# The first load of a decode kernel, w1, issued as two loads: 16 partitions and 112

## The chip, the cores and the metric

The kernel runs on one core of a Trainium2 chip. Its time is the device time of one execution in microseconds; the figure before the change is the median of three runs, 343.58 us (343.47 to 343.65). The profile is of one more execution, taken by the hardware profiler.

A core has a matrix engine (TensorE, PE in the profile; PEld is its weight load), a vector engine (VectorE, DVE), a scalar engine (ScalarE, ACT), a general one (GpSimd, POOL) and a sequencer that here only issues transfers (SyncE, SP). Transfers from device memory (HBM) into the on-chip memory (SBUF, 128 partitions) are run by 16 DMA engines. Each queue of transfers, such as SP's, spreads a transfer over them.

## The reference

One decode step for two sequences (B = 2, one new token each, model width 512). A gate mixes an attention block and a feed-forward block:

```
g = sigmoid((x * gate_w).sum(-1))                       # one number per sequence
q = x @ wq                                              # 512 -> 32 heads x 128
p = softmax(q . k_cache^T / sqrt(128))                  # 32 heads, 4096 cached rows each
a = (p @ v_cache) @ wo                                  # 4096 -> 512
b = relu(x @ w1) @ w2                                   # 512 -> 1376 -> 512
out = g * a + (1 - g) * b
```

All inputs are bfloat16. The K cache and the V cache hold 2 x 32 x 4096 x 128 numbers, 67 MB each; wq and wo have 4 MB each, w1 and w2 1.4 MB each. Every byte is read once.

## The kernel before, in words

The program is written engine by engine. A small class collects, for each engine, a list of operations with the markers or load semaphores they wait for; nothing is reordered afterwards, so every engine and every queue works in the order in which its list was filled.

SBUF holds one large tile `kv` of five regions (A, Ah, B, Bh, C), each 128 partitions of 16,384 bfloat16. Everything large that is loaded passes through it. A *piece* is a half region or two halves of a K or V unit: 4096 KB in one region or 8192 KB in two (128 partitions with one contiguous run of 32 or 64 KB each). w1 lies at the head of region B (128 partitions, 4 x 1376 numbers each, 11,008 bytes), wq in region C.

SP's list is, in order: w1 (L331), wq (L332), ten pieces of K and nine of V (L335), the 96 rows of w2 that don't fit the regular form (L338, two loads of 12 partitions each), wo in two loads (L340, L342), the rest of w2 in three loads (L344), and at the end the store of the result (L346). A load waits on SP until the last reader of its region is done. The first ones need no wait: w1, wq, the first half unit of K (region Bh) and the next unit (regions A and Ah). The third piece goes to region B and waits for the last matmul that reads w1 (marker `pe_h`); the fourth goes to region C and waits for `pe_q`, the end of the projection that reads wq. ACT's queue issues two tiny loads at the start, x (two partitions, L329) and the gate's row (one partition, L330).

The work at the start: PE turns x and the gate's row (function `gate`, L353), and a chain of short DVE and ACT operations computes the gate. `ffn_h` (L445 and after) clears a PSUM area on DVE and then runs 24 matmuls of x against w1, the first of which waits for w1's semaphore and for the clear. `ffn_relu` follows on DVE. `q_proj` waits for wq, computes q, turns it and lays it out (ACT copies, then POOL products). After that the K loop runs: DVE transposes a quarter piece as soon as the piece has landed (L477), PE takes the scores (L504, L483). Softmax, the V loop (L617, L483), and the output projections with w2 and wo follow.

Loads and compute are tied by counting semaphores. A load adds 16 to its semaphore when it is complete; w1's semaphore is `sem["w1"]`, and the only one who waits for it is the first matmul of `ffn_h`.

Of the kernel before, what the change touches and what calls it, by code (L numbers as in the profile page):

```python
# [122 lines left out]
def bass_gated_mix__gqa_block_cached__dense_activation_relu__decode_kernel(  # L123
# [34 lines left out]
    w1 = kv[:, REGION["B"]:REGION["B"] + 4 * DFF]  # L158
# [41 lines left out]
    def psf(p0, p1, c0, n):  # L200
        return PSF[p0:p1, c0:c0 + n]
# [22 lines left out]
    sem = {n: nc.alloc_semaphore("sem_" + n) for n in names}  # L224
# [9 lines left out]
    def marker(name):  # L234
        m = mk.get(name)
        if m is None:
            m = _Marker()
            mk[name] = m
        return m
# [29 lines left out]
    def dve(fn, waits=(), signal=None, dwaits=()):  # L269
        P.add("dve", fn, waits=[marker(w) for w in waits], signal=marker(signal) if signal else None, dwaits=dwaits)  # L270

    def act(fn, waits=(), signal=None, dwaits=()):
        P.add("act", fn, waits=[marker(w) for w in waits], signal=marker(signal) if signal else None, dwaits=dwaits)

    def pe(fn, waits=(), signal=None, dwaits=()):
        P.add("pe", fn, waits=[marker(w) for w in waits], signal=marker(signal) if signal else None, dwaits=dwaits)
# [5 lines left out]
         waits=["c_i16z"], signal="c_i16")  # L282
# [11 lines left out]
         waits=["c_s1"], signal="c_s2")  # L294
    pool(lambda g: g.affine_select(out=sell_odd, in_=sell_odd, pattern=[[4, 8], [32, 4]],
                                   compare_op=ALU.is_ge, fill=0.0, base=3, channel_multiplier=-1),
         waits=["c_s2"], signal="c_sell")
# [3 lines left out]
         waits=["c_m1"], signal="c_m2")  # L301
    pool(lambda g: g.affine_select(out=mask8[:], in_=mask8[:], pattern=[[16, 8]],
                                   compare_op=ALU.is_ge, fill=0.0, base=15, channel_multiplier=-1),
         waits=["c_m2"], signal="c_mask8")
# [3 lines left out]
         waits=["c_s4z"], signal="c_s4")  # L308
# [3 lines left out]
    w1_in = B_w1.rearrange("(p t) f -> p (t f)", t=4)  # L312
# [13 lines left out]
    def sp(fn, waits=(), dwaits=()):  # L326
        P.add("sp", fn, waits=waits, dwaits=dwaits)

    act(lambda e: e.dma_start(x_sb[0:2, :], A_x.rearrange("b s d -> (b s) d")).then_inc(sem["x"], 16))  # L329
    act(lambda e: e.dma_start(x_sb[2:3, :], gate_w.rearrange("(o d) -> o d", o=1)).then_inc(sem["gw"], 16))  # L330
    sp(lambda e: e.dma_start(w1, w1_in).then_inc(sem["w1"], 16))  # L331
    sp(lambda e: e.dma_start(wreg[:, :], wq_in).then_inc(sem["wq"], 16))  # L332
    for kind, n, u, halves, region in pieces:
        sp(lambda e, kind=kind, n=n, u=u, halves=halves, region=region:
           e.dma_start(piece_sb(halves, region), piece_in(kind, u, halves)).then_inc(landed[kind, n][0], 16),  # L335
           waits=[marker(m) for m in predecessor[kind, n]])
    for a in range(2):
        sp(lambda e, a=a: e.dma_start(w2x[32 * a:32 * a + 12, :, :].rearrange("p j n -> p (j n)"), w2x_in[a]).then_inc(sem["w2x"], 16),  # L338
           waits=[marker("c_w2x")])
    sp(lambda e: e.dma_start(wreg[:, 0:512 * WO_CUT], wo_in[:, 0:512 * WO_CUT]).then_inc(sem["wo0"], 16),  # L340
       waits=[marker(holder["C"][0])])
    sp(lambda e: e.dma_start(wreg[:, 512 * WO_CUT:HALF], wo_in[:, 512 * WO_CUT:HALF]).then_inc(sem["wo1"], 16))  # L342
    for name, r0, r1 in (("w2b", 0, 7), ("w2c", 7, 9), ("w2d", 9, 10)):
        sp(lambda e, name=name, r0=r0, r1=r1: e.dma_start(w2[:, r0:r1, :], w2_in[:, r0:r1, :]).then_inc(sem[name], 16),  # L344
           waits=[marker(holder["Ah"][0])])
    sp(lambda e: e.dma_start(out.rearrange("b s (k n) -> (b s k) n", k=2), out_sb[:, :]).then_inc(sem["out"], 16),  # L346
       dwaits=[(sem["fin"], 2)])
# [55 lines left out]
    def x_rows(e, out, c, t, rhs, held):  # L403
        if held:
            return mm_held(e, out, xTw[:, t, :], rhs, t == 0, t == 3, (128, 32), (0, 32 * c))
        return e.matmul(out, lhsT=xTw[:, t, :], rhs=rhs, start=(t == 0), stop=(t == 3), tile_position=(0, 32 * c))  # L406
# [37 lines left out]
    def ffn_h():  # L444
        dve(lambda v: v.memset(psf(0, 128, HR_C0, 448), 0.0), signal="dve_h0")  # L445
        for t in range(4):
            for c in range(4):
                def fn(e, t=t, c=c):
                    rhs = w1[:, t * DFF + 96 + 320 * c:t * DFF + 416 + 320 * c].rearrange("p (i j) -> p j i", j=10)
                    out = psf(32 * c, 32 * c + 32, HR_C0, 320).rearrange("p (j i) -> p j i", j=10)  # L450
                    return x_rows(e, out, c, t, rhs, False)
                first = t == 0 and c == 0
                pe(fn, dwaits=([(sem["w1"], 16)] if first else []), waits=(["dve_h0"] if first else []))
                if c < 2:
                    def fnx(e, t=t, c=c):
                        rhs = w1[:, t * DFF + 48 * c:t * DFF + 48 * c + 48].rearrange("p (i e j) -> p j e i", i=4, e=3)
                        out = psf(32 * c, 32 * c + 32, HR_C0 + 320, 128).rearrange("p (j k) -> p j k", j=4)[:, :, 0:12].rearrange(
                            "p j (e i) -> p j e i", e=3)
                        return x_rows(e, out, c, t, rhs, True)
                    pe(fnx)  # L460
        P.ops["pe"][-1].marker = marker("pe_h")
# [269 lines left out]

    gate()
    ffn_h()
    ffn_relu()
    q_proj()
# [73 lines left out]
```

## Time and profile before

| What | us |
|---|---|
| median of three runs | 343.58 |
| the profiled execution's own time | 343.51 |
| its span, first to last instruction | 342.2 |
| PE busy | 228.1 (67%) |
| DVE busy | 197.4 (58%) |
| ACT busy | 9.9 (3%) |
| POOL busy | 14.2 (4%) |
| issue of w1 on SP to its landing | 5.6 |
| issue of wq on SP to its landing | 14.8 |

The span is shorter than the execution's own time by what lies before the first and after the last instruction. An engine's busy time leaves out instructions that only issue a transfer; those appear in the timeline as SPq and ACTq, with the time that the issuing takes. "To landing" runs from the start of an issue to the moment when the load is complete. In a table by stretches, each row gives a stretch (start and end from the span's start, its length), the busy time and number of instructions of PE, PEld, DVE, ACT and POOL, the granted clock of TensorE as a share of full speed, the mean busy share of the 16 DMA engines and the GB/s that they moved. A packet's time and bytes are put down at the packet's start, so that share can go over 1 in a short stretch. Behind these tables lie the trace's packet records: start, length and bytes of every packet, with its queue but not with its engine.

### The profile page before, as it was taken

Reading aid. Unit: us, or ns where it says so; the run is one execution under the profiler, and the core shown is the slowest. Engines: PE = TensorE matmul, PEld = TensorE weight load, DVE = VectorE, ACT = ScalarE, POOL = GpSimd, SP = SyncE. Lnnn points to the kernel's source line nnn. Section 1 sums busy time; section 2 is a strip of 40 time slices with the busy share of each in tenths; the row PEclk is TensorE's granted clock in tenths of the full one; section 3 lists DMA queues with packets and bytes.
Section 4 is the critical chain, followed back from the end, with each engine's and each line's share of the span. In section 5 each row is a group of like instructions: output and inputs, shape, how many; then the busy total and the mean of one; then the engine's idle time right before and its main releaser. Section 6 shows DMA issues by size and latency. Waiting matters only on the chain.

```text
span 342.2 us, 2434 instructions
## 1 busy us (share of the span) xinstructions
PE 228.1 (67%) x1279; PEld 54.0 (16%) x770; DVE 197.4 (58%) x139; ACT 9.9 (3%) x29; POOL 14.2 (4%) x41
## 2 busy tenths in 40 slices
PE   0467329799969799689799463809172552909976
PEld 0111001111111111111111120202020110202313
DVE  1239059899889899698999496140606032020621
ACT  1051000000000000000000110000000000000000
POOL 6000000000000000000000200000000000000000
PEclk9999959989989899999999967856769585767999
DMA  8998989899999999898989999999989999989995
GB/s 349 429 490 370 483 375 483 371 486 414 444 467 391 426 433 483 383 475 375 483 383 475 398 467 423 429 467 391 483 383 475 391 467 391 467 387 433 426 421 241
DMA packets 3793, 145.50 MB, mean 425 GB/s; under 512 B 429, under 2 KB 564, under 8 KB 844
## 3 DMA queue, kind: packets, MB, share of 16 engines
q1 hardware_dynamic: 3782, 145.43, 98.6%
q8 instruction: 4, 0.07, 0.1%
q14 instruction: 1, 0.01, 0.0%
q10 hardware_dynamic: 6, 0.00, 0.0%
HBM read 145.43 MB, written 0.00 MB: 425 GB/s over the span
## 4 chain that ended last, share of the span: by engine, by line
DMA 63%; DVE 19%; PE 15%; issue 2%; ACT 0%; SPq 0%; DVEq 0%
DMA kv<-in_A_k_cache_dram 32%; DMA kv<-in_A_v_cache_dram 24%; DVE kt L477 17%; DMA kv<-in_B_w_dram 7%; PE PS L483 6%; PE PS L617 4%; PE PS L504 2%; PE PS L588 1%; DVE mpad L520 1%; ACT kt L532 0%; DVE kt L536 0%; DVE kt L549 0%; PE PS L697 0%; PE PS L516 0%; SPq L332 0%
## 5 line engine op out<-in xcount | busy, mean ns | idle before, releaser
L477 DVE STREAM_TRANSPOSE kt<-kv 128x2048 f32<-128x2048 f32 x64 | 141.2, 2274 | 25.7 <-DMA kv<-in_A_k_cache_dram 25.7
L504 PE MATMUL PS<-kt,qbuf 128*128 128x512 bf16 x256 | 106.2, 415 | 31.3 <-issue 23.0
L483 PE MATMUL PS<-kt,qbuf 128*128 128x512 bf16 x256 | 106.1, 415 | 0.0
L617 PE MATMUL PS<-kv,kt 128*64 128x512 bf16 x192 | 47.4, 471 | 55.2 <-DMA kv<-in_A_v_cache_dram 55.2
L629 DVE TENSOR_TENSOR kt<-PS,maskc 32x512 f32<-32x512 f32 (+1 forms) x21 | 14.5, 689 | 88.3 <-PE PS L483 81.3
L504 PEld LDWEIGHTS PS<-kt,qbuf 128*128 128x128 bf16 x256 | 25.7, 100 | 140.7 <-issue 140.7
L483 PE MATMUL PS<-kv,kt 128*64 128x512 bf16 x192 | 46.8, 465 | 0.0
L617 PEld LDWEIGHTS PS<-kv,kt 128*64 128x64 bf16 x192 | 15.2, 135 | 96.1 <-issue 96.1
L561 DVE TENSOR_TENSOR kt<-kt,mask 128x2048 bf16<-128x2048 bf16 (+1 forms) x10 | 16.2, 1656 | 0.0
L588 PE MATMUL PS<-kv,kt 128*32 128x512 bf16 x128 | 8.9, 432 | 8.6 <-DVE kt L549 7.3
L401 POOL TENSOR_TENSOR qbuf<-qs,mask 128x64 bf16<-128x64 bf16 x16 | 6.5, 406 | 160.7 <-PE PS L483 141.1
L641 DVE TENSOR_REDUCE kt<-kt 128x128 f32<-128x512 f32 x9 | 9.2, 1025 | 0.3
L483 PE MATMUL PS<-qbuf,ident 128*32 128x512 bf16 x37 | 9.0, 379 | 0.0
L406 PE MATMUL PS<-kv,xTw 128*32 128x320 bf16 (+1 forms) x32 | 5.3, 691 | 5.2 <-DMA kv<-in_A_wq_dram 3.2
L532 ACT ACTIVATE kt<-PS,negm 128x512 bf16<-128x512 f32 x4 | 2.7, 686 | 168.9 <-DVE negm L528 168.9
L588 PEld LDWEIGHTS PS<-kv,kt 128*32 128x32 bf16 x128 | 3.9, 107 | 15.6 <-DVE kt L549 7.8
L430 DVE CAST qrow<-PS 128x256 bf16<-128x256 f32 x2 | 2.6, 1524 | 5.7 <-PE PS L483 5.7
L729 ACT ACTIVATE out_sb<-PS 4x128 bf16<-4x128 f32 x1 | 0.3, 267 | 142.3 <-PE PS L712 142.3
L353 PE MATMUL PS<-ident,x_sb 3*128 3x3 bf16 x4 | 0.3, 166 | 6.2 <-DMA x_sb<-in_gate_w_dram 6.2
L520 DVE TENSOR_REDUCE mpad<-PS 128x2 f32<-128x2048 f32 x1 | 2.3, 2292 | 3.1 <-PE PS L516 3.1
L356 DVE COPY xT<-PS 128x12 bf16<-128x12 bf16 x1 | 0.2, 171 | 6.5 <-PE PS L353 6.5
L483 PE MATMUL PS<-kv,xTw 128*32 128x512 bf16 (+1 forms) x24 | 3.7, 511 | 0.0
(88 smaller groups left out, 53.6 us busy)
## 6 DMA issues: line engine op xcount, KB each, us to landing
kv<-in_A_k_cache_dram SPq DMA_DIRECT2D x4, 4096.0 KB, 29.4
kv<-in_A_v_cache_dram SPq DMA_DIRECT2D x2, 4096.0 KB, 23.5
kv<-in_A_wq_dram SPq DMA_DIRECT2D x1, 4096.0 KB, 14.8
kv<-in_A_wo_dram SPq DMA_DIRECT2D x1, 3072.0 KB, 33.4
kv<-in_B_w_dram SPq DMA_DIRECT2D x1, 1376.0 KB, 5.6
kv<-in_A_wo_dram SPq DMA_DIRECT2D x1, 1024.0 KB, 35.4
kv<-in_B_w_dram SPq DMA_DIRECT2D x1, 896.0 KB, 22.3
kv<-in_B_w_dram SPq DMA_DIRECT2D x1, 256.0 KB, 22.6
```

Source lines behind the costliest of these rows:

```text
L401: pool(lambda g: g.tensor_tensor(out=out, in0=src, in1=mask, op=ALU.mult).then_inc(sem_q[k % 2], 1), waits=waits)
L406: return e.matmul(out, lhsT=xTw[:, t, :], rhs=rhs, start=(t == 0), stop=(t == 3), tile_position=(0, 32 * c))
L477: dve(lambda v: v.transpose(out=dst, in_=pairs[:, h, 64 * a:64 * a + 64, :]).then_inc(sem_kt[i % SPAN], 1), waits=([f"pe_sc_{i - NKT}"] if ...
L483: return e.add_instruction(mybir.InstMatmult(start_tensor_calc=start, stop_tensor_calc=stop, tile_size=size, tile_position=at, ldweights=F ...
L504: ins = e.matmul(out, lhsT=lhsT, rhs=rhs, start=False, stop=False)
L520: dve(lambda v: v.tensor_reduce(out=mpad[:, 0:2], in_=psf(0, 128, 0, 4 * BANK).rearrange("p (par n) -> p par n", par=2), axis=AX.X, op=ALU ...
L532: act(lambda a, g=g, par=par: a.activation(out=E_sb[:, 32 * g:32 * g + 32, 16 * par:16 * par + 16], in_=psf(0, 128, (2 * par + g) * BANK, ...
L561: ins = v.tensor_tensor(out=out, in0=src.unsqueeze(2).to_broadcast(shape), in1=mask8[:].unsqueeze(1).unsqueeze(3).to_broadcast(shape), op= ...
L588: ins = e.matmul(psf(32 * t, 32 * t + 32, V_BS[n] * BANK, 512), lhsT=v_weights(n)[:, j], rhs=rows[:, :, j, :], start=(j < 4), stop=(j >= n ...
L617: ins = e.matmul(out, lhsT=lhsT, rhs=rows[:, :, k, :], start=start, stop=stop, tile_position=(0, 64 * t))
L629: dve(lambda e: e.tensor_tensor(out=parts[p0:p1], in0=psf(p0, p1, bank * BANK, 512).rearrange("p (c d) -> p c d", c=4), in1=maskc[p0:p1].u ...
L641: dve(lambda e: e.tensor_reduce(out=X2[:, b, k, :], in_=parts.rearrange("p c d -> p d c"), axis=AX.X, op=ALU.add), waits=[f"dve_m{n}"], si ...
```

## The change

The load of w1 is issued as two loads by SP, one right after the other: first partitions 0 to 15, then partitions 16 to 127. Source and destination rows are those of before; both loads add 16 to the same semaphore, and the matmul that waits for w1 waits for 32 instead of 16. As the change's author describes it, the first of the two is one packet for each DMA engine. All other issues keep their order behind these two.

```diff
     act(lambda e: e.dma_start(x_sb[0:2, :], A_x.rearrange("b s d -> (b s) d")).then_inc(sem["x"], 16))
     act(lambda e: e.dma_start(x_sb[2:3, :], gate_w.rearrange("(o d) -> o d", o=1)).then_inc(sem["gw"], 16))
-    sp(lambda e: e.dma_start(w1, w1_in).then_inc(sem["w1"], 16))
+    sp(lambda e: e.dma_start(w1[0:16], w1_in[0:16]).then_inc(sem["w1"], 16))
+    sp(lambda e: e.dma_start(w1[16:128], w1_in[16:128]).then_inc(sem["w1"], 16))
     sp(lambda e: e.dma_start(wreg[:, :], wq_in).then_inc(sem["wq"], 16))
...
                 first = t == 0 and c == 0
-                pe(fn, dwaits=([(sem["w1"], 16)] if first else []), waits=(["dve_h0"] if first else []))
+                pe(fn, dwaits=([(sem["w1"], 32)] if first else []), waits=(["dve_h0"] if first else []))
```

## The prediction

> **What bounds the kernel now.** I read the page's table of DMA queues first, because the kernel reads 145 MB.
>
> ```profile
> q1 hardware_dynamic: 3782, 145.43, 98.6%
> HBM read 145.43 MB, written 0.00 MB: 425 GB/s over the span
> ```
>
> The columns are packets, MB and the share of 16 DMA engines' span. The one queue that SP fills keeps all 16 engines busy for 98.6% of 342.2 us. Nothing else on the page comes near (PE 67%, DVE 58%), so bytes set the time, at 425/16 = 26.6 GB/s for each engine. I call one engine a lane: it works through its own part of every load in order, and a lane that starts late stays late: in the packet records the sixteen lanes finish w1 spread over 0.42 us, wq over 0.45 and the first K piece over 0.45.
>
> Next, whether a delay at the head reaches the end: the DMA issues, with size and median time from issue to landing, and the first long piece of the chain that ended last (start, length).
>
> ```profile
> kv<-in_B_w_dram SPq DMA_DIRECT2D x1, 1376.0 KB, 5.6
> kv<-in_A_wq_dram SPq DMA_DIRECT2D x1, 4096.0 KB, 14.8
> kv<-in_A_v_cache_dram SPq DMA_DIRECT2D x7, 28.5
> kv<-in_A_k_cache_dram SPq DMA_DIRECT2D x6, 28.4
> ```
>
> ```profile
> 1.72 24.08 DMA kv<-in_A_k_cache_dram
> ```
>
> A full K or V piece has 8192 KB, which is 19.7 us at 425 GB/s; it lands 28.4 us after its issue. So 8.7 us of older loads still lie in the queue at each issue, the engines never wait for SP, and a later start of the stream moves every landing, every release of a buffer and the end by the same amount. The start counts one for one.
>
> The start itself: first SP's timeline (start, length, instruction), then the stretches of the first 5 us (last two columns: DMA share and GB/s, both put down where a packet starts).
>
> ```profile
> 0.80 0.40 SPq L331 DMA_DIRECT2D kv<-in_B_w_dram  x1
> 1.26 0.41 SPq L332 DMA_DIRECT2D kv<-in_A_wq_dram  x1
> ```
>
> ```profile
> 1.70:1.80 0.10, 0.00 (x0) 0.00 (x0) 0.00 (x0) 0.10 (x1) 0.10 (x3) 1.00 0.07 21
> 1.80:2.20 0.40, 0.00 (x0) 0.00 (x0) 0.00 (x0) 0.40 (x1) 0.40 (x3) 1.00 1.49 275
> 2.20:3.00 0.80, 0.00 (x0) 0.00 (x0) 0.00 (x0) 0.71 (x1) 0.80 (x1) 1.00 0.64 220
> 3.00:4.00 1.00, 0.00 (x0) 0.00 (x0) 0.00 (x0) 0.00 (x0) 1.00 (x2) 1.00 1.01 429
> 4.00:5.00 1.00, 0.00 (x0) 0.00 (x0) 0.00 (x0) 0.00 (x0) 0.87 (x8) 1.00 0.96 407
> ```
>
> w1 is 128 rows of 11,008 bytes, a packet each, eight a lane. From 4 to 5 us 407 KB go, which is 37 packets in 0.96 x 16 us of lane time: 0.415 us a packet, 3.32 us for eight. The start is slower: from 1.80 to 3.00 us 110 + 176 KB start, 26 packets. Sixteen lanes at full pace from 1.80 would have started 48 (three each). The 22 missing are 1.4 a lane, 0.57 us. This is what the edit can work on.
>
> **The change, part by part.** The sum is against the profiled execution's 343.51 us (span 342.2 and 1.3 around it), which lies 0.07 below the median 343.58.
>
> *One more issue on SP.* 0.40 us and a gap of 0.06: wq, all K, V and later loads are issued 0.46 later. It costs nothing by itself: wq's packets have to wait for w1's, which fill the lanes to about 5.5 us, and wq's issue would move from 1.26 to 1.72. The first release that SP waits for is that of region B by the feed-forward matmuls at 13.0 us, so no one waits for SP.
>
> *The wait for w1 counts to 32.* One PE wait still, and it is not the last one: w1 lands at 0.80 + 5.6 = 6.4 us, while the first matmul of L406 starts at 10.12, released by the DVE memset at 9.64. Up to 3.7 us of delay of w1 are hidden there. Behind it PE has done at 12.95 and then waits for wq until 16.12, so 3.2 us cover the gate's row too, which comes between w1's packets. The waits later in the kernel are on loads that move along.
>
> *The first piece, 16 rows.* The bounds from rows are far apart. If each of 16 lanes takes one row at its own pace, it costs 0.415 us, what the same row costs now. The two rows of x, in neighbouring partitions, are the row for that: they start together in the stretch 1.70:1.80, and 0.07 x 16 x 0.10 us is some 0.11 us of lane time for both with their completions, 44 ns a row in the packet records, no slower than the 46 ns of a 1,024-byte packet of w2 late in the run. The other bound is the only load near in shape, w2's extra rows (L338: 12 partitions, twice 48 KB). The packet records show its 24 packets of 4,096 bytes from 325.05 to 326.48 us, three at a time, 156 ns apart in each row of eight: 12 partitions got three lanes' worth, 3 x 26.3 GB/s, four partitions to a lane. By that 16 partitions get four lanes' worth, and the piece takes 4 x 0.415 = 1.66 us instead of 0.415 (1.92 if I divide the 98,304 bytes by the whole 1.43 us and scale from 12 partitions to 16). I take 1.66: w2's extra rows are near in partitions (12 against 16) and in bytes (96 KB against 172), while x's 44 ns are too short to show a jam.
>
> [...]
>
> *The second piece, 112 rows.* Seven a lane would be 7 x 0.415 = 2.91 us. [...] So the whole of w1 on a full group goes from 3.32 to 1.66 + 3.32 us: **+1.66**.
>
> *The faster start.* The first piece has 16 packets to lay out instead of 128, so its lanes may start together and up to 0.1 earlier (x's first packet started at 1.71, w1's at 1.82). At most the 0.57 + 0.10 = 0.67 us of the slow start go; nothing goes if the second piece's packets come in the same slow manner 0.46 us later. I take the middle, **-0.33**, as there is no row of a 16-row load.
>
> Sum: 1.66 - 0.33 = +1.33, so 343.51 + 1.33 = **344.84 us**, 0.4% over the median. From these terms alone: 344.1 (first piece 1.66, the full start gain, and the second piece's eighth row hidden: 1.66 - 0.67 - 0.41 = 0.58) to 345.4 (first piece 1.92, no start gain).
>
> **The rivals.** *The first piece goes at full width.* Sixteen lanes take a row each in 0.415 us, then seven. The second issue comes 0.46 later, and the packet that is already done covers 0.415 of it: +0.05 if the slow start only moves to the second piece, -0.33 if half of it goes. 343.2 to 343.6 us, no measurable change. For it: x's rows. Against it: w2's extra rows. That the split then does nothing to the time is this same case.
>
> *Faster by over 0.2%* (0.69 us, about what a measurement of this kernel can tell from no change). The slow start at 1.8 to 3.0 us would have to vanish whole and a little more, 343.51 - 0.75 = 342.8 us. It decides at whether the second piece's packets lie on every lane when its first row is done, at 1.71 + 0.415 = 2.13 us. Against it: w1's first packet came 1.02 us after its issue, and an issue at 1.26 puts the second piece's first at 2.28. For it: x's first packet came 0.91 after its issue.
>
> [...]
>
> **How the numbers follow.** Forecast 0.55, full width 0.32, faster 0.05, jam in both pieces 0.08. The range 343.2 to 345.7 us leaves out the faster case, the jam and a little of the full-width case's lower edge. Slower by over 0.2% is the forecast and the jam less 0.03 for the forecast's lower edge (344.1, where 0.2% over the median is 344.27): 0.60. Faster is 0.05, and the rest, 0.35, is within 0.2%.
>
> **What would show it.** The first 16 packets in the changed kernel's trace: near 1.6 us long, or four lanes' worth of GB/s until about 3.5 us, if I am right; near 0.4 us and over 300 GB/s by 2.5 us if full width is right. wq's landing (16.06 now) and the end of the first K wait (25.80 now) should move by 1.3 us, and the last wait for w2 (339.39) by as much; a shift that differs between them would break the one-for-one step. The forecast is wrong if few partitions do not slow the lanes, or if the slow start of the first 1.2 us is what the 128 packets cost and goes whole.

## The result and the profile after

The changed kernel takes 345.48 us (median of six runs, 345.45 to 345.65) where the kernel before takes 343.62 in the same comparison (343.47 to 343.70): 1.0055 times as long, 95% interval 1.0042 to 1.0068, so 1.9 us or 0.55% slower. The profiled execution took 345.45 us, its span is 344.2.

The page's DMA queues first (packets, MB, share of 16 engines' span), as before:

```profile
q1 hardware_dynamic: 3798, 145.43, 98.6%
HBM read 145.43 MB, written 0.00 MB: 423 GB/s over the span
```

Same bytes, 16 packets more (the completions of one more load), the same 98.6%, and 423 GB/s where it was 425. The engines are as busy as they were; some of that time moves less.

Where it does is in the stretches of the first 9 us of the changed kernel (last two columns: DMA share and GB/s, put down at a packet's start):

```profile
1.80:2.20 0.40, 0.00 (x0) 0.00 (x0) 0.00 (x0) 0.40 (x1) 0.40 (x3) 1.00 1.61 385
2.20:3.00 0.80, 0.00 (x0) 0.00 (x0) 0.00 (x0) 0.71 (x1) 0.80 (x1) 1.00 1.29 208
3.00:4.00 1.00, 0.00 (x0) 0.00 (x0) 0.00 (x0) 0.00 (x0) 1.00 (x2) 1.00 0.70 198
4.00:5.00 1.00, 0.26 (x4) 0.21 (x4) 0.29 (x3) 0.00 (x0) 0.87 (x8) 1.00 0.81 231
5.00:6.00 1.00, 0.59 (x2) 0.50 (x2) 0.28 (x3) 0.00 (x1) 0.79 (x6) 1.00 1.01 297
6.00:7.00 1.00, 0.00 (x0) 0.00 (x0) 0.73 (x3) 0.17 (x1) 0.85 (x2) 1.00 1.21 341
7.00:8.00 1.00, 0.00 (x0) 0.00 (x0) 0.91 (x6) 0.00 (x0) 0.26 (x2) 1.00 1.51 546
8.00:9.00 1.00, 0.23 (x4) 0.17 (x6) 0.35 (x1) 0.00 (x0) 0.00 (x0) 1.00 0.99 426
```

The first 0.4 us are better than before (385 GB/s against 275): the lanes do start sooner and together (the first sixteen packets from 1.82 to 2.25 us, before to 2.56). Then, from 3 to 6 us, the rate is 200 to 300 GB/s where it was 407 and more, and full speed is back only when w1 is through (its last packet ends at 7.91 us; the 546 of the stretch before 8 us come from the long packets of wq, whose bytes all count where they start). The DMA issues (size, time from issue to landing) say which load was held up:

```profile
kv<-in_A_wq_dram SPq DMA_DIRECT2D x1, 4096.0 KB, 16.6
kv<-in_B_w_dram SPq DMA_DIRECT2D x1, 1204.0 KB, 7.4
kv<-in_B_w_dram SPq DMA_DIRECT2D x1, 172.0 KB, 3.6
```

The 172 KB of the first piece were issued at 0.80 us and landed at 4.4; in the packet records its last packet ends at 2.94, so 1.46 us pass between the last packet and the landing, against 0.4 for w1 before (last packet 6.01, landing 6.4). The first sixteen packets overlap (the last starts at 2.25 us, the first ends at 2.51), so sixteen lanes took a row each. The trace also records the 16 additions to a load's semaphore one by one. All 16 of the first piece come between 3.76 and 4.44 us, so every lane was held up; for w1 before, they come 0.36 us on average after the lanes' last packets. The second piece, issued at 1.25, landed at 8.65.

From there the shift runs through the kernel. The long waits of the chain that ended last (start, length), at its head and at its end, first before, then after, with the matmul that the last wait of the changed kernel releases:

```profile
37.55 28.33 DMA kv<-in_A_k_cache_dram
...
85.86 28.42 DMA kv<-in_A_k_cache_dram
...
317.01 22.33 DMA kv<-in_B_w_dram
```

```profile
2.20 25.86 DMA kv<-in_A_k_cache_dram
...
40.15 27.73 DMA kv<-in_A_k_cache_dram
...
87.86 28.44 DMA kv<-in_A_k_cache_dram
...
319.48 21.80 DMA kv<-in_B_w_dram
```

```profile
341.33 1.17 PE L698 MATMUL PS<-kv,hT 128*4 128x128 bf16 x36 [0.69 <-DMA kv<-in_B_w_dram]
```

These waits end at 28.06, 67.88, 116.30 and 341.28 us; before, they ended at 25.80 (the row of 24.08 us in the prediction), 65.88, 114.28 and 339.34. The delay is 2.26 us at the head and 1.94 to 2.02 from the second wait on.

The packet records give the ledger. They don't name the lane, so each line is the mean over 16 packets in order of start, before and after:

```
packets of w1             before          after           lane later by
first 16, mean end        2.93 us         2.67 us         -0.26
second 16, mean end       3.34            3.86            +0.51
last 16, mean end         5.83            7.54            +1.71
length, third to last     0.413           0.56 to 0.64
first 16 of wq, length    1.22            1.42
```

So there are three items: a start that is 0.26 us better, 0.77 us lost on the packet that follows the first piece, and 1.20 us lost on the six after it, which take some 0.62 us instead of 0.413. wq's first packets take the last 0.20.

### The profile page after: what moved, and what is told of

Read it like the earlier page. It is cut to its first block, busy times and chain, and to the rows that moved or that the text cites. A ratio compares the mean times of both kernels' runs of the same rounds, so it can differ in the third digit from the quotient of the medians.

```text
span 344.2 us, 2435 instructions
## 1 busy us (share of the span) xinstructions
PE 229.2 (67%) x1279; PEld 54.3 (16%) x770; DVE 197.5 (57%) x139; ACT 9.9 (3%) x29; POOL 14.2 (4%) x41
## 3 DMA queue, kind: packets, MB, share of 16 engines
q1 hardware_dynamic: 3798, 145.43, 98.6%
## 4 chain that ended last, share of the span: by engine, by line
DMA 63%; DVE 19%; PE 15%; issue 2%; ACT 0%; SPq 0%; DVEq 0%
DMA kv<-in_A_k_cache_dram 32%; DMA kv<-in_A_v_cache_dram 24%; DVE kt L478 17%; DMA kv<-in_B_w_dram 6%; PE PS L484 6%; PE PS L618 4%; PE PS L505 2%; PE PS L589 2%; DVE mpad L521 1%; ACT kt L533 0%; DVE kt L537 0%; DVE kt L550 0%; PE PS L698 0%; PE PS L517 0%; SPq L333 0%
## 5 line engine op out<-in xcount | busy, mean ns | idle before, releaser
L505 PE MATMUL PS<-kt,qbuf 128*128 128x512 bf16 x256 | 107.7, 421 | 30.2 <-issue 22.4
L484 PE MATMUL PS<-kt,qbuf 128*128 128x512 bf16 x256 | 107.6, 420 | 0.0
L589 PE MATMUL PS<-kv,kt 128*32 128x512 bf16 x128 | 9.6, 451 | 8.1 <-DVE kt L550 7.3
L537 DVE STREAM_TRANSPOSE kt<-kt 128x1024 bf16<-128x1024 bf16 x2 | 2.5, 1240 | 1.5 <-ACT kt L533 1.5
L407 PEld LDWEIGHTS PS<-kv,xTw 128*32 128x32 bf16 x32 | 1.2, 126 | 13.6 <-DMA kv<-in_A_wq_dram 7.6
```

Source lines behind the costliest of these rows:

```text
L484: return e.add_instruction(mybir.InstMatmult(start_tensor_calc=start, stop_tensor_calc=stop, tile_size=size, tile_position=at, ldweights=F ...
L505: ins = e.matmul(out, lhsT=lhsT, rhs=rhs, start=False, stop=False)
L589: ins = e.matmul(psf(32 * t, 32 * t + 32, V_BS[n] * BANK, 512), lhsT=v_weights(n)[:, j], rhs=rows[:, :, j, :], start=(j < 4), stop=(j >= n ...
```

## The experiments

The theory was that lanes that write into few partitions share their way in. The rivals were that any second load at the start costs, and that the read side dislikes the new blocks of rows. The edits are shown against the kernel before; where w1 comes in two loads, the matmul waits for 32 as in the change.

**Cut in halves.** A milder cut in two equal loads:

```diff
-    sp(lambda e: e.dma_start(w1, w1_in).then_inc(sem["w1"], 16))
+    sp(lambda e: e.dma_start(w1[0:64], w1_in[0:64]).then_inc(sem["w1"], 16))
+    sp(lambda e: e.dma_start(w1[64:128], w1_in[64:128]).then_inc(sem["w1"], 16))
```

> w1 as two loads of 64 partitions each (0 to 63, then 64 to 127). Theory (lanes that write into few partitions share their way in): each half puts two lanes on each group of eight partitions, packets take about 0.83 us instead of 0.415, w1 takes 6.6 us of every lane instead of 3.3, less some 0.3 us of faster start: 346.6 us, more than the 345.48 of the change although the cut is milder. Rival (a second load at the start costs, whatever its width): the same as the change, 345.5. Rival (the read side dislikes blocks of seven rows): blocks of four rows a lane are harmless, 343.6.

Measured: 346.93 us against 343.74, ratio 1.0091 [1.0074, 1.0108], +3.2 us. The stretch from 3.50 to 8.00 us (GB/s in the last column), first of this kernel, then of the next one:

```profile
3.50:8.00 4.50, 0.85 (x6) 0.71 (x6) 0.91 (x7) 0.17 (x1) 3.28 (x15) 1.00 1.09 228
```

**Cut by columns.** Two loads again, both over all partitions:

```diff
-    sp(lambda e: e.dma_start(w1, w1_in).then_inc(sem["w1"], 16))
+    sp(lambda e: e.dma_start(w1[:, 0:DFF], w1_in[:, 0:DFF]).then_inc(sem["w1"], 16))
+    sp(lambda e: e.dma_start(w1[:, DFF:4 * DFF], w1_in[:, DFF:4 * DFF]).then_inc(sem["w1"], 16))
```

> w1 as two loads of all 128 partitions, the first quarter of each row and then the rest. Theory (few partitions): nothing shares, one more issue on SP is hidden, 343.4 to 343.9 us. Rival (a second load at the start costs, whatever its width): about 345.5.

Measured: 343.73 us against 343.74, ratio 1.0001 [0.9991, 1.0011].

```profile
3.50:8.00 4.50, 0.85 (x6) 0.71 (x6) 2.13 (x12) 0.17 (x1) 3.28 (x15) 1.00 1.02 435
```

With busy engines in both (shares of 1.09 and 1.02), 64 partitions at a time move 228 GB/s and 128 move 435. Half of the halves' packets take 0.84 to 0.89 us, twice 0.413; most of the others take 0.7 to 0.83. That two lanes meet on each eight partitions, as the theory's estimate has it, no record shows. A second load costs nothing when it is wide, and the halves cost more than the change although neither of them is as narrow as 16: two issues are not the cause, and blocks of seven rows are not needed for a loss.

**16 rows more, narrow.** The first piece's price by itself, away from the start: w1 as before, and behind it an extra load into 16 partitions of a tile that is free until 25 us, with bytes that nobody reads.

```diff
     sp(lambda e: e.dma_start(w1, w1_in).then_inc(sem["w1"], 16))
+    sp(lambda e: e.dma_start(kt_late[0:16, 0:4 * DFF], w1_in[0:16]).then_inc(sem["px"], 16))
...
-            waits=([f"pe_sc_{i - NKT}"] if i >= NKT else ["dve_h2"] if i == 2 else []), dwaits=([landed["k", n]] if first else []))
+            waits=([f"pe_sc_{i - NKT}"] if i >= NKT else ["dve_h2"] if i == 2 else []), dwaits=(([landed["k", n]] if first else []) + ([(sem["px"], 16)] if i == 0 else [])))
```

The second edit makes the first writer of that tile wait for the extra load. It stands in all kernels with an extra load and is left out below; the load has landed long before 25 us.

> w1 as before, and right behind it an extra load of its first 16 rows (172 KB) into 16 partitions of a tile that is still unused; the extra bytes are not read. Theory: the piece takes 4 x 0.415 = 1.66 us of all lanes, 343.6 + 1.66 = 345.3 us. Rivals (start or read side): 0.41 us, 344.0.

Measured: 345.61 us against 343.74, ratio 1.0058 [1.0041, 1.0074], +1.87 us.

**The same bytes, wide.**

```diff
+    sp(lambda e: e.dma_start(kt_late[:, 0:688], B_w1[0:64, :].rearrange("a (b c) -> (a b) c", c=688)).then_inc(sem["px"], 16))
```

> The same extra 172 KB as in the run before, but spread over 128 partitions (1,376 bytes each). All theories: 0.41 to 0.5 us for the bytes, 344.0 to 344.1 us. If it costs as much as the narrow one, width is not the cause.

Measured: 344.18 us against 343.74, ratio 1.0014 [1.0004, 1.0023], +0.44 us. The issues of the two extra loads and of w1 in front of them, first narrow, then wide (size, issue to landing):

```profile
kv<-in_B_w_dram SPq DMA_DIRECT2D x1, 1376.0 KB, 6.9
...
kt<-in_B_w_dram SPq DMA_DIRECT2D x1, 172.0 KB, 7.2
```

```profile
kv<-in_B_w_dram SPq DMA_DIRECT2D x1, 1376.0 KB, 5.8
...
kt<-in_B_w_dram SPq DMA_DIRECT2D x1, 172.0 KB, 5.7
```

172 KB into 16 partitions cost 1.87 us, into 128 partitions 0.44; both read the same bytes of w1, so narrowness costs 1.43. The narrow load lands 1.5 us later, and even w1 in front of it lands 1.1 us later. By the theory, a lane that is still writing its last rows of w1 shares its way with those that have gone on to the 16 partitions; that the lanes meet in this way is argued, as no record tells which lane writes where.

**112 rows more.** The second piece's price by itself, and the same number of bytes over 128 partitions, meant to be read from places that are as far apart from lane to lane:

```diff
+    sp(lambda e: e.dma_start(kt_late[16:128, 0:4 * DFF], w1_in[16:128]).then_inc(sem["px"], 16))
```

> w1 as before, and right behind it an extra load of its rows 16 to 127 (1204 KB) into partitions 16 to 127 of a tile that is still unused; the extra bytes are not read. Theory (lanes of seven neighbouring rows meet in the same groups of partitions): packets of 0.62 us as in the changed kernel, 7 x 0.62 = 4.3 us, 347.9 us. Rival (the 0.62 us came only from the backlog of the 16-row piece in front): 7 x 0.415 = 2.9 us, 346.5. Rival (read side dislikes lanes 77 KB apart): 347.9 too, told apart by the next run.

```diff
+    sp(lambda e: e.dma_start(kt_late[:, 0:4816], B_w1[0:448, :].rearrange("a (b c) -> (a b) c", c=688).rearrange("(p x) c -> p (x c)", x=7)).then_inc(sem["px"], 16))
```

> The same number of extra bytes (1204 KB) over 128 partitions, 9,632 bytes each, so that eight rows of one lane again span 77,056 bytes of the source, as seven rows of 11,008 do. Theory: 2.9 us, 346.5 us. Rival (read side): 4.3 us, 347.9.

Measured: 348.18 against 343.68 us for the 112 partitions, ratio 1.0129 [1.0112, 1.0146], +4.50 us; 346.59 against 343.68 for the 128, ratio 1.0085 [1.0068, 1.0101], +2.91. The same stretch of both, 112 partitions first (DMA share and GB/s in the last two columns):

```profile
6.60:8.00 1.40, 0.40 (x5) 0.34 (x5) 0.57 (x4) 0.00 (x0) 0.64 (x2) 1.00 0.98 275
```

```profile
6.60:8.00 1.40, 0.65 (x6) 0.59 (x6) 0.57 (x4) 0.00 (x0) 0.64 (x2) 1.00 0.99 420
```

The DMA share is the same 0.98 and 0.99, and 275 GB/s come out of it instead of 420. So 112 partitions, seven rows a lane, cost 1.59 us by themselves, with nothing narrow in front of them, and the wide load costs just its bytes (7 x 0.415 = 2.9). This speaks against the read side, but less firmly than it was meant to: that a lane takes neighbouring rows, and so the same distance in the source, is assumed, and the records don't show it. Nor does a run tell what it is about these 112 partitions: their number, seven rows a lane, or the start at partition 16.

**wq first.** Does the slow start belong to w1's small packets?

```diff
-    sp(lambda e: e.dma_start(w1, w1_in).then_inc(sem["w1"], 16))
     sp(lambda e: e.dma_start(wreg[:, :], wq_in).then_inc(sem["wq"], 16))
+    sp(lambda e: e.dma_start(w1, w1_in).then_inc(sem["w1"], 16))
```

> w1 whole as before, but issued after wq. It asks whether the slow start (0.57 us of lane time lost before 3 us) belongs to the small packets of w1: wq's packets have 32 KB and last 1.2 us, so lanes that got one are busy until the next are there. If so, 343.3; if the loss is that lanes start at different times, no change, 343.6. The later w1 delays the feed-forward matmuls to about 16.4 us, which nothing waits for before the third K piece.

Measured: 343.84 us against 343.68, ratio 1.0004 [0.9995, 1.0014]. No gain: wq's first sixteen packets took 1.48 to 2.13 us instead of 1.21, so a slow start is paid with wq in front too.

**The narrow piece in front, and the change in the other order.** The parts cost 1.43 and 1.59 us, 3.0 together, but the change costs 1.9. Two more kernels ask where the rest went. First the extra 16 rows in front of w1 instead of behind it:

```diff
+    sp(lambda e: e.dma_start(kt_late[0:16, 0:4 * DFF], w1_in[0:16]).then_inc(sem["px"], 16))
     sp(lambda e: e.dma_start(w1, w1_in).then_inc(sem["w1"], 16))
```

> The extra 16-row load (172 KB, bytes not read) in front of the whole w1 instead of behind it. In the changed kernel's packet records the first piece costs its lanes 0.77 us on the second packet and brings its first packets 0.26 us earlier; behind w1 the same load cost 1.87. If the start hides part of the narrow load's cost (lanes wait there anyway for the next load's packets): 0.41 for the bytes + 0.77 - 0.26 = 0.9 us, 344.6. If the start hides nothing: 345.5, as behind w1.

Then the two loads of the change, swapped:

```diff
-    sp(lambda e: e.dma_start(w1, w1_in).then_inc(sem["w1"], 16))
+    sp(lambda e: e.dma_start(w1[16:128], w1_in[16:128]).then_inc(sem["w1"], 16))
+    sp(lambda e: e.dma_start(w1[0:16], w1_in[0:16]).then_inc(sem["w1"], 16))
```

> The change with its two loads in the other order: partitions 16 to 127 first, then 0 to 15. If the start hides part of the narrow piece, it does so no longer: 1.4 us for the 112 rows' own jam and 1.43 for the narrow piece in the middle of the stream (e3 less e4), 343.65 + 2.8 = 346.5. If the order makes no difference: 345.5.

Measured: 344.55 us against 343.67 for the first, ratio 1.0027 [1.0017, 1.0037], +0.88; 346.31 against 343.67 for the second, ratio 1.0076 [1.0059, 1.0093], +2.64, near the 2.8 expected. In front the narrow load costs 0.88 us, behind w1 1.87: the place is worth 1.0 us. That the start hides this much, because the lanes wait there anyway, is the likely reason; that other packets come behind it (w1's of 11 KB, not wq's of 32 KB) was not varied by itself. In the records of the kernel with 16 rows in front, w1's own packets have a mean of 1.03 us at first, then 0.46, then 0.42, so what a narrow load leaves behind is nearly over after one packet; the 0.62 us of the change's second piece are that piece's own. The parts now add up: 0.88 less 0.44 for the bytes, and 1.59, make 2.0, and the change measures 1.9. Each of these prices has an interval of 0.3 to 0.6 us to either side, so the sum shows that nothing large is missing, not that it fits to a tenth.

## Why the prediction was right

The time lay in its range (343.2 to 345.7), and on the predicted side: +1.86 us by the medians against +1.33 forecast from the profiled execution. The mechanism, few partitions slow the lanes, was right; that the sum came this close is partly luck. 345.48 us is over the 345.4 that the forecast's own terms reach, and 0.64 us from 344.84.

- *One more issue costs nothing.* Right: two wide loads take 343.73 us against 343.74.
- *The first piece, 1.66 us instead of 0.415.* The mechanism, few partitions are jammed, is shown: 1.87 us against 0.44 in the middle of the stream. But its place was oversized. The change shows 0.77 us of the 1.24 that the step took over the old price, and the rest probably goes by while the lanes wait at the start anyway. The row that the price came from, w2's extra rows, used three lanes (three packets of 4,096 bytes at a time, 0.16 us each, and three additions to the semaphore when each of its loads lands); the change used sixteen, and all sixteen landed late (3.76 to 4.44 us). So the price was near (1.66 us forecast, 1.87 measured in the middle of the stream), but it does not show as packets of four times the length. x's two rows, which spoke for full width, indeed said nothing.
- *The second piece, 3.32 us, 0.41 over seven packets at full pace.* No run shows the 3.32 us of a full group, and this is the term that failed by most: the 112 rows alone cost 1.59 us more than the same bytes wide. The jam in both pieces, with its chance of 0.08, was there in addition to the forecast's other terms, not instead of them: the sixteen lanes run at two thirds of their pace (some 0.62 us a packet instead of 0.413). Why 112 partitions do that is not shown.
- *The faster start, -0.33.* Right in size: -0.26 in the packet records. The first 16 packets end at 2.67 us on average in both kernels that begin with the narrow piece, against 2.93 to 3.13 in the five that begin with the whole w1.
- *What would show it.* I said that the first 16 packets would be near 1.6 us long. They took 0.42 to 0.89, which read by itself would have spoken for full width. The jam is in the landing (1.46 us after the last packet) and in the packets that follow.
- *The wait for w1 is not the last one.* Wrong, without effect. The gate's row, one packet between w1's, ran at 2.64 us instead of 5.28, so the gate's work was done sooner and the first feed-forward matmul then did wait for w1, 2.80 us, to start at 8.77 instead of 10.12. Two rows of before, then the same two after, where the lines count one more:

```profile
10.12 0.76 PE L406 MATMUL PS<-kv,xTw 128*32 128x320 bf16 x4 [2.04 <-DVE PS L445]
16.12 0.62 PE L406 MATMUL PS<-kv,xTw 128*32 128x512 bf16 x4 [3.18 <-DMA kv<-in_A_wq_dram]
```

```profile
8.77 0.76 PE L407 MATMUL PS<-kv,xTw 128*32 128x320 bf16 x4 [2.80 <-DMA kv<-in_B_w_dram]
18.39 0.62 PE L407 MATMUL PS<-kv,xTw 128*32 128x512 bf16 x4 [6.76 <-DMA kv<-in_A_wq_dram]
```

The last line shows why that earlier start is worth nothing: the next matmuls wait for wq until 18.39, 2.27 us later than before.

- *One for one to the end.* Right, with one thing to add. I said that a shift that differs between the signs would break this step, and they differ: wq's landing and the first K wait move by 2.26 us, the next waits by 2.0, the last by 1.94. But the mean of the 16 additions to a semaphore moves by 2.04 to 2.06 us in each load behind w1 but the extra rows of w2. So the lanes keep their delay to the end. A reader waits for the last of the 16, and how far that one is behind the mean changes: for wq and the first K piece by 0.2 us before and 0.4 after, which gives the 2.26; for the load of w2 that ends the chain by 1.04 before and 0.94 after, which gives the 1.94. From the second K piece to the end the last lane is 0.9 to 1.5 us behind the mean, probably the one held up by the instruction fetch of 16 KB that the records have at 27.7 us before (1.02 us long) and at 29.6 after (1.10).

The forecast's total came near because one term, the first piece, was too large by 0.47 us and another, the second piece, too small by about 1.0 (1.20 on its packets and 0.20 on wq's first, against 0.41).

No kernel here beats the one before; the best of the others, columns, is level with it.

## What to carry to other kernels

When the DMA engines bound a kernel, cut a load along its columns, if at all, and leave all 128 partitions in every part: here two such parts cost nothing, two halves of the partitions 3.2 us on 1.4 MB. Count what is left after a cut too: 112 partitions cost 1.59 us more than their bytes as an extra load, and in the change they were the larger part of the loss (1.20 us on six packets). To price a narrow load, put it into the stream as an extra load beside an equally large wide one; its own packet records did not show here what it costs (0.42 to 0.89 us each, for a load that lands 1.46 us after the last).

## What was unexpected of the hardware

The load into 16 partitions had ordinary packets (0.42 to 0.89 us in the change, against 0.41 to 1.31 for the first sixteen before) and landed 1.46 us after the last of them; the lost time appeared in the records of whatever comes next on the lanes (1.05 us on average for the packet behind it instead of 0.44). The DMA share was 0.98 while the 112 partitions jammed, and 1.09 in the halves, so a busy share near one does not tell that the engines run at full rate; GB/s over the same stretch does (275 against 420, 228 against 435).

At the start of the stream a narrow load cost 1.0 us less than its 1.87 behind w1. Neither smaller first packets (2,752 bytes, the columns) nor larger ones (32 KB, wq first) shortened the start to any effect on the time: 343.73 and 343.84 us.
